# First rows and weights loaded ahead of the filter, and TensorE's dummy matmuls on a preset constant

## The chip, the core and the metric

The kernel runs on one core of a Trainium2 chip. The metric is the time of one execution on the device in microseconds (us). A core has TensorE (PE in the profile; its weight loads are PEld), VectorE (DVE), ScalarE (ACT), GpSimd (POOL) and SyncE (SP). SP and ACT issue the DMAs, which 16 DMA engines carry out.

## The reference

```
x  = A_q                                   # 2048 rows of 512, bf16
xn = layernorm(x)
k_shift = sum over 4 taps of shifted k * shift_k
kv = k_shift * v
y  = causal convolution of kv with ssm_k along the 2048 rows, by FFT of length 4096
y  = y + kv * ssm_D
s  = xn * y
g  = silu( (gelu(xn @ w_gate) * (xn @ w_up)) @ w_down )    # 512 -> 1792 -> 512
out = x + s * g
```

## The kernel before

**Tiling.** The 2048 rows are held as 16 tiles of 128 rows (X), in four quarters q of four tiles. Each quarter goes through layernorm (`ln(q)`: stats, aggregate, variance, a power on POOL, normalise into XN), a transpose into xnT (`xn_transpose(q)`), 14 feed-forward units (`unit(q, m)`: four gate and four up matmuls, gelu on ACT, a product on DVE into HT) and the down projection (`down(q)`). For quarter 0 the layernorm works tile by tile, and units 0 and 1 (`N_HALF = 2`) are split: matmuls of 128 columns on one row tile each, gelu and product on halves.

**The convolution** runs beside it, as a two-stage Fourier transform on PE. The filter `ssm_k` (Hn, four chunks h0 to h3) is transposed on PE (`h_transpose`, L915, in f32) into HTr, goes through stage 1 (L958) and is stored to a DRAM tensor ZH by ACT's queue, and reloaded as BH for stage 2 (L1027). The values kv go the same way (L949, ZK, BK). Spectra are multiplied on DVE, transformed back (L1027, ZI, BI, L1277), and joined to the result in the tail. The transform's tables (F, TF and their transposes) are computed at the start by POOL (iota), DVE (phases) and ACT (sine).

**Dummy matmuls.** `warm_up` issues `N_WARM` matmuls on a zeroed tile (ZERO, in AST) before PE has real work; their result is never read. The same step of DVE (`zero`) sets COLS, the bias of the sine, and clears ZERO, which a later small load (kz) also reads.

**Order.** Every step is a task with a number, in the order in which the program adds it. `SEQ` is a list written out by hand: it names the tasks in the order in which they are issued, each engine taking its own in that order; a `b` behind a number takes the second of two engines that could do the step (for copies out of PSUM, DVE in place of ACT). `Sched.run` only hands out buffers along that list, by estimated times; `LAND` holds the estimated landings of the loads. A recording layer (`Trk`) adds the semaphore waits. `ORDER` is the order in which SP issues the input loads: x00 and x01 are the first two pairs of row tiles, w0 the gate and up weights of units 0 and 1 (wg0, wu0), D the row `ssm_D`, s0 the taps.

**Names that the prediction uses.** L614 is the DMA helper, L632 and L635 the copies out of PSUM on ACT and DVE, L641 every plain matmul (dummies, gate, up, down), L671 to L689 POOL's iotas and identity matrices, L695 and L696 the two memsets of `zero`, L720 to L734 DVE's table phases, L744 and L748 the sine, and the gelu table behind it, L848 the stats, L849 the aggregate, L858 and L859 the variance on ACT or DVE, L861 the power on POOL, L870 the normalise step on DVE, L891 the transposes of XN, L915 those of the filter.

Of the kernel before, what the change touches and what calls it, by code (L numbers as in the profile page):

```python
# [6 lines left out]
BF16 = mybir.dt.bfloat16  # L7
# [14 lines left out]
NB = 2  # L22
LN_EPS = 1e-5
TURN = 8192
N_WARM = 12
ORDER = "x00 h0 x01 w0 D0 h1 w1 h2 h3 s0 k0 w2 x1 k1 k2 w3 d0 d1 v0 v1 k3 v2 v3 x2 x3"
SEQ = (
# [22 lines left out]
)  # L50
NF_BANKS = 4
ISSUE = 470.0
LAND = {"x0_0": 4400, "h0": 5900, "x0_1": 7000, "D": 4000, "wg0": 7950, "wu0": 8800, "h1": 10100, "wg1": 11600, "wu1": 13100, "h2": 14450, "h3": 15750, "sk": 17800, "kh1": 19200, "kh113": 19400, "kz": 10800, "k0": 20600, "wg2": 22500, "wu2": 24050, "x1": 25400, "k1": 26750, "k2": 28100, "wg3": 29650, "wu3": 31200, "wd0": 33450, "wd1": 35700, "v0": 37050, "v1": 38400, "k3": 39750, "v2": 41100, "v3": 42450}
W_XT, W_SW, W_BK, W_BH, W_ZI, W_BI, W_ZK, W_MI, W_G1 = 765000, 735000, 667000, 688000, 274000, 714000, 690000, 329000, 150000
NC_PAIRS = 4
SMALL = 1.15 * 262144
# [25 lines left out]
class Trk:  # L82
# [29 lines left out]
    def res(self, name, ap):  # L112
        t = ap.tensor
        tn = type(t).__name__
        if tn.startswith("SB"):
            key = "SB"
            addr = self.nc.lookup_mloc(t).addr
        else:
            assert tn.startswith("PS")
            key = "PS:" + t.name  # L120
            addr = 0
        esz = mybir.dt.size(ap.dtype)
        pairs = [list(q) for q in ap.ap]
        pst, pn = pairs[0]
        pstart = ap.offset // pst if pst else 0
        inner = ap.offset - pstart * pst
        hi = sum(st * (n - 1) for st, n in pairs[1:])
        r = Res(name, key, pstart, pstart + pn, addr + inner * esz, addr + (inner + hi + 1) * esz)
        lst = self.res_by_key.setdefault(key, [])
        for o in lst:  # L130
            if o.plo < r.phi and r.plo < o.phi and o.blo < r.bhi and r.blo < o.bhi:
                o.ovl.append(r)
                r.ovl.append(o)
        lst.append(r)
        return r
# [278 lines left out]
def build_kernel(nc, A_q, A_k, A_v, A_shift_k, A_ssm_k, A_ssm_D, B_w_gate, B_w_up, B_w_down, out):  # L414
    with ExitStack() as es0:
# [100 lines left out]
        trk = Trk(nc, block)  # L516
        S = Sched()
        res = trk.res

        def dsem(name):  # L520
            return DSem(nc.alloc_semaphore(name), name)
# [4 lines left out]
        def bank(b):  # L526
            return PSALL[:, 512 * b.slot:512 * (b.slot + 1)]
# [4 lines left out]
        def R_bank(b):  # L532
            return [R_ps[b.slot // 2][b.slot % 2]]
# [79 lines left out]
        def dma(eng, out_ap, in_ap, sem, r, w):  # L613
            trk.dma(eng, lambda e: e.dma_start(out=out_ap, in_=in_ap), sem, r=r, w=w)  # L614
# [3 lines left out]
        def load(name, out_ap, in_ap, w_res, w_buf, nbytes, ring="SP", r=(), rb=()):  # L618
            sem = dsem("d_" + name)
            last_load[0] = S.add([("loads", ISSUE)], lambda e: dma(ring, out_ap, in_ap, sem, r, w_res), r=rb, w=w_buf, nbytes=nbytes, land=float(LAND[name]))  # L620

# [18 lines left out]
        def mm(h, o, l, r, st, sp):  # L640
            return h.matmul(o, lhsT=l, rhs=r, start=st, stop=sp)  # L641
# [9 lines left out]
        bF1, bG1, bMF, bMI, bid, bSKB = B("F1"), B("G1"), B("TF"), [B(f"MI{i}") for i in range(2)], B("id"), [B(f"SKB{j}") for j in range(4)]  # L651
# [39 lines left out]
        ZERO = AST[:, 0, 0, 0, :]  # L691
        R_zero = res("ZERO", ZERO)
        bwarm = B("warm")
# [2 lines left out]
            trk.op("DVE", lambda h: h.memset(ZERO, 0.0), w=[R_zero])  # L696
        t_zero = S.add([("DVE", 330.0)], zero, w=[bwarm])
        warm = B("pswarm", pF)

        def warm_up(e):  # L700
            for i in range(N_WARM):
                trk.op("PE", lambda h: mm(h, bank(warm), ZERO[:, 0:128], ZERO, True, True), r=[R_zero], w=R_bank(warm), accum=True)

        t_warm = S.add([("PE", 10 * 427.0 + (N_WARM - 10) * 217.0)], warm_up, r=[bwarm], w=[warm])
        bcq, bck, bid32 = B("cq"), B("ck"), B("id32")
        S.add([("POOL", 420.0)], lambda e: pool_q(), w=[bcq])
        S.add([("POOL", 1000.0)], lambda e: pool_k(), w=[bck])
# [47 lines left out]
        bFP, bQ, bMQ, bMF2 = B("fp"), B("q"), B("mq"), B("mf2")  # L755
# [2 lines left out]
        S.add([("DVE", 360.0)], lambda e: f_phase(), r=[bFM], w=[bFP])  # L758
        def f_sin(e):
            sin(F1[:], C32[:].rearrange("p a c -> p (a c)"), [R_C32], R_F1)  # L760
        S.add([("ACT", 510.0)], f_sin, r=[bFP, bcq], w=[bF1])
        S.add([("DVE", 800.0)], lambda e: m_parts(), r=[bcq], w=[bQ])
        bTAB = B("tab")
        t_mq = S.add([("DVE", 900.0)], lambda e: m_phase(), r=[bQ, bck], w=[bMQ])
# [70 lines left out]

        for what in ORDER.split():
            if what[0] == "x" and len(what) == 3:
# [87 lines left out]
        for k in range(KD):  # L925
# [4 lines left out]
                    r=[bHD, *[bHTr[k][0] for k in range(KD)]], w=[bFold], rr=[R_D, *R_HTr[0]], ww=R_HTr[0])  # L930
# [369 lines left out]
        for j in range(6):  # L1300
# [7 lines left out]
                  r=[b2], w=[B(f"out{j}")], nbytes=262144)  # L1308
# [55 lines left out]
```

## Time and profile before

| | us |
|---|---|
| median of 3 runs | 188.87 (188.80 to 188.93) |
| profiled execution, its own time | 189.08 |
| span of its profile, first to last instruction | 187.3 |
| PE busy | 182.4 (97%) |
| DVE busy | 164.9 (88%) |
| ACT busy | 141.1 (75%) |
| POOL busy | 10.9 (6%) |

A line of the timeline is: start in us, duration in us, engine, source line, operation, tile written <- tiles read, shape, count of equal instructions merged, and in brackets how long the engine stood idle before it and what ended that. The duration of a merged line runs from the first start to the last end. A line of the chain holds start, duration and what it was. Ends of matmuls are modelled, so starts are what PE's rows are read by. A line of DMA issues ends with the size and the median time from issue to landing.

### The profile page before, as it was taken

Reading aid. Unit: us, or ns where it says so; the run is one execution under the profiler, and the core shown is the slowest. Engines: PE = TensorE matmul, PEld = TensorE weight load, DVE = VectorE, ACT = ScalarE, POOL = GpSimd, SP = SyncE. Lnnn points to the kernel's source line nnn. Section 1 sums busy time; section 2 is a strip of 40 time slices with the busy share of each in tenths; the row PEclk is TensorE's granted clock in tenths of the full one; section 3 lists DMA queues with packets and bytes.
Section 4 is the critical chain, followed back from the end, with each engine's and each line's share of the span. In section 5 each row is a group of like instructions: output and inputs, shape, how many; then the busy total and the mean of one; then the engine's idle time right before and its main releaser. Section 6 shows DMA issues by size and latency. Waiting matters only on the chain.

```text
span 187.3 us, 3717 instructions
## 1 busy us (share of the span) xinstructions
PE 182.4 (97%) x1474; PEld 81.5 (44%) x1474; DVE 164.9 (88%) x250; ACT 141.1 (75%) x196; POOL 10.9 (6%) x26
## 2 busy tenths in 40 slices
PE   7899999999999999999999999999999999999993
PEld 2675544534343334334444433433343344445552
DVE  7899999999999999978689689998999972759695
ACT  3847896997879799799638897998999663424871
POOL 5401402000000000022000000000000000000000
PEclk9999999999999999999999999999999999999999
DMA  5999999999584986457989997499445163995056
GB/s 188 318 381 294 371 379 365 400 411 319 163 321 159 336 290 223 158 195 238 311 244 233 321 332 240 153 304 307 182 168 168 60 216 123 321 392 187 0 205 243
DMA packets 36422, 47.84 MB, mean 255 GB/s; under 512 B 7347, under 2 KB 26039, under 8 KB 36406
## 3 DMA queue, kind: packets, MB, share of 16 engines
q1 hardware_dynamic: 29878, 39.23, 62.8%
q10 hardware_dynamic: 6528, 8.39, 13.0%
q8 instruction: 11, 0.18, 0.4%
q14 instruction: 5, 0.04, 0.2%
HBM read 27.39 MB, written 14.68 MB: 225 GB/s over the span
## 4 chain that ended last, share of the span: by engine, by line
PE 90%; DVE 4%; DMA 3%; issue 0%; SPq 0%; ACT 0%
PE psall L641 73%; PE psall L1027 6%; PE psall L1223 3%; DMA X<-in_A_q_dram 3%; PE psall L949 2%; PE psall L958 2%; PE psall L915 2%; PE psall L1277 1%; DVE G L1306 1%; DVE G L1245 1%; DVE G L1244 1%; PE psall L891 1%; DVE G L1294 1%; SPq L614 0%; DVE XN L1294 0%
## 5 line engine op out<-in xcount | busy, mean ns | idle before, releaser
L641 PE MATMUL psall<-xnT,Wu 128*128 128x512 bf16 (+1 forms) x248 | 55.8, 359 | 0.0
L641 PE MATMUL psall<-xnT,Wg 128*128 128x512 bf16 (+1 forms) x248 | 55.1, 359 | 0.7 <-DVE xnT L635 0.7
L641 PE MATMUL psall<-Wd,HT 128*128 128x512 bf16 (+1 forms) x182 | 40.6, 368 | 0.0
L1193 ACT ACTIVATE GE<-psall 128x512 bf16<-128x512 f32 x54 | 31.4, 604 | 12.1 <-PE psall L641 11.3
L1202 DVE TENSOR_TENSOR HT<-psall,GE 128x512 bf16<-128x512 f32 x43 | 29.0, 687 | 11.0 <-PE psall L641 10.8
L641 PEld LDWEIGHTS psall<-xnT,Wu 128*128 128x128 bf16 x248 | 22.5, 98 | 25.9 <-issue 2.3
L641 PEld LDWEIGHTS psall<-xnT,Wg 128*128 128x128 bf16 x248 | 21.7, 98 | 27.0 <-issue 2.3
L632 ACT ACTIVATE BO<-psall 128x1024 bf16<-128x1024 f32 x22 | 22.1, 1023 | 9.3 <-PE psall L1277 4.3
L641 PEld LDWEIGHTS psall<-Wd,HT 128*128 128x128 bf16 x182 | 16.1, 98 | 20.9 <-issue 3.7
L1130 DVE TENSOR_TENSOR HSW<-KB,HSW 128x2048 bf16<-128x2048 bf16 x16 | 19.2, 1218 | 0.0
L632 ACT ACTIVATE HSW<-psall 128x1024 bf16<-128x1024 f32 x16 | 15.5, 1035 | 2.3 <-PE psall L1027 2.2
L632 ACT ACTIVATE KB<-psall 128x1024 bf16<-128x1024 f32 x14 | 13.8, 1028 | 2.6 <-PE psall L1027 2.4
L1010 DVE TENSOR_TENSOR KAC<-KAC,KTM 128x2048 bf16<-128x2048 bf16 x12 | 14.7, 1224 | 0.1
L1008 DVE TENSOR_TENSOR KTM<-KK,SKB 128x2048 bf16<-128x2048 bf16 x12 | 14.7, 1222 | 0.1
L632 ACT ACTIVATE AST<-psall 128x1024 bf16<-128x1024 f32 x12 | 12.3, 1024 | 1.9 <-PE psall L949 1.5
L1223 PE MATMUL psall<-Wd,HT 128*64 128x512 bf16 (+1 forms) x112 | 12.3, 366 | 0.0
L848 DVE BATCH_NORM_STATS2 stats<-X 128x6 f32<-128x512 bf16 x16 | 10.6, 672 | 0.2
L1130 DVE TENSOR_TENSOR KB<-KB,HSW 128x2048 bf16<-128x2048 bf16 x8 | 9.6, 1219 | 0.1
L1153 DVE TENSOR_TENSOR HSW<-HSW 128x2048 bf16<-128x2048 bf16 x8 | 9.5, 1219 | 0.0
L1234 ACT ACTIVATE G<-psall 128x512 bf16<-128x512 f32 x12 | 6.9, 599 | 3.2 <-PE psall L641 3.2
L861 POOL TENSOR_TENSOR mv<-mv,NHALF 128x1 f32<-128x1 f32 (+1 forms) x7 | 5.3, 756 | 68.7 <-DVE mv L859 65.0
L1236 DVE SCALAR_TENSOR_TENSOR G<-G,psall 128x512 bf16<-128x512 bf16 x12 | 8.0, 681 | 1.2 <-ACT G L1234 1.2
(91 smaller groups left out, 177.8 us busy)
## 6 DMA issues: line engine op xcount, KB each, us to landing
BH<-ZH SPq DMA_DIRECT2D x8, 512.0 KB, 5.6
BK<-ZK SPq DMA_DIRECT2D x8, 512.0 KB, 6.1
HSW<-HSW SPq DMA_DIRECT2D x16, 256.0 KB, 3.4
ZI<-BO ACTq DMA_DIRECT2D x16, 256.0 KB, 2.6
BI<-ZI SPq DMA_DIRECT2D x8, 512.0 KB, 7.4
ZK<-AST SPq DMA_DIRECT2D x6, 512.0 KB, 3.4
Hn<-in_A_ssm_k_dram SPq DMA_DIRECT2D x4, 512.0 KB, 7.3
KK<-in_A_k_dram SPq DMA_DIRECT2D x4, 512.0 KB, 10.7
```

Of the source, the lines that this page charges most:

```text
L632: return h.activation(o, i, ACTF.Copy, scale=scale)
L641: return h.matmul(o, lhsT=l, rhs=r, start=st, stop=sp)
L848: t_stats[t] = op([("DVE", 670.0)], lambda e, h, t=t: h.bn_stats(stats[:, t, :], X[:, t, :]), r=[bX[q][t % 4]], w=[bst[t]], rr=[R_X[t]], w ...
L1008: op([("DVE", dur)], lambda e, h, j=j, m=m: h.tensor_tensor(KTM[:, m.slot, :, :], kk(j), sk(j), ALU.mult), r=need + [bSKB[j], a], w=[m], r ...
L1010: op([("DVE", dur)], lambda e, h, m=m: h.tensor_tensor(KAC[:, a.slot, :, :], KAC[:, a.slot, :, :], KTM[:, m.slot, :, :], ALU.add), r=[m], ...
L1027: trk.op("PE", lambda h: h.matmul(ps(s, i)[b, :], lhsT=wt(col)[a, :], rhs=data(col)[a, :], start=n < 16, stop=n >= len(todo) - 16, tile_po ...
L1130: return hd.tensor_tensor(pair(KB, *(2 * DM * z for z in slots())) if to else x, k, x, ALU.mult)
L1153: return hd.tensor_tensor(x, x, y, ALU.add)
L1193: op([("ACT", act(512))], lambda e, h: h.activation(GE[:, g.slot, :], bank(pg), ACTF.Gelu_apprx_tanh), r=[pg], w=[g], rr=lambda: R_bank(pg ...
L1202: op([("DVE", dve(512, 1))], lambda e, h: h.tensor_tensor(HT[:, q % 2, m, :], bank(pu), GE[:, g.slot, :], ALU.mult), r=[pu, g], w=[bHT[q][m]],
L1223: trk.op("PE", lambda h, m=m, i=i, c=c: h.matmul(pc()[c, :], lhsT=HT[:, q % 2, m, 128 * jt + 64 * i:128 * jt + 64 * i + 64], rhs=Wd[:, m, ...
L1236: op([("DVE", dve(512, 1))], lambda e, h, g=g, pc=pc: h.scalar_tensor_tensor(out=g, in0=g, scalar=1.0, in1=pc(), op0=ALU.add, op1=ALU.mult ...
```

## The change

The loads are issued as x00, x01, w0, D, h0, w1, h1, h2, h3 instead of x00, h0, x01, w0, D0, h1, w1, h2, h3; from the taps on the order is the same. The dummies read a constant tensor of ones, one value on each partition, read 512 and 128 times by a step of 0; the program's preamble sets it before the engines are released, so they wait for no step of DVE. There are 13 of them instead of 12. The sine of table F now names the memset of COLS among the steps that it follows. `LAND` takes new estimates, and the first 260 of `SEQ`'s 816 entries stand in a new order; from `120 180 160 141 162 119 121 129 545` on it is the old list.

What the new list does to the engines' programs, up to there: PE goes from the dummies to the transposes of the first two row tiles, to gate and up of units 0 and 1 on the first of them, and comes to the filter's transposes afterwards, in seven groups of four or eight instead of six. DVE begins with L720, then does the memsets and the other table steps, and takes the stats of the third tile between the normalise steps of the first and the second. DVE copies three PSUM tiles fewer (8 instead of 11 plain copies) and computes one variance fewer; ACT takes them (197 activations instead of 193). Four of ACT's filter stores (ZH), not two, stand ahead of the copies of the second quarter's transposes. On POOL the bf16 identity comes before the f32 one; on SP the transpose of F comes before that of the first half of TF.

```
-N_WARM = 12
-ORDER = "x00 h0 x01 w0 D0 h1 w1 h2 h3 s0 k0 w2 x1 k1 k2 w3 d0 d1 v0 v1 k3 v2 v3 x2 x3"
+N_WARM = 13
+ORDER = "x00 x01 w0 D0 h0 w1 h1 h2 h3 s0 k0 w2 x1 k1 k2 w3 d0 d1 v0 v1 k3 v2 v3 x2 x3"
 SEQ = (
-    "0 2 3 16 1 17 18 10 4 6 48 19 20 5 21 7 22 23 8 9 24 25 26 11 49 27 28 29 67 68 76b 30 31 32 65 66 73 12 77 78 74 75 69 87 91 86 90b 365 366 70 79b 71 "
+    "2 7 0 8 3 9 10 11 16 4 17 65 66 5 67 1 68 6 76 73b 74 75 12 86 69 18 77 78 90 87 365 70 377 79b 19 71 367 72 91 80 20 379 82b 378 81 381 21 366 88 92 "
...
-LAND = {"x0_0": 4400, "h0": 5900, "x0_1": 7000, "D": 4000, "wg0": 7950, "wu0": 8800, "h1": 10100, "wg1": 11600, "wu1": 13100, "h2": 14450, "h3": 15750, ...
+LAND = {"x0_0": 3800, "h0": 8050, "x0_1": 4900, "D": 6750, "wg0": 5850, "wu0": 6700, "h1": 12450, "wg1": 9600, "wu1": 11100, "h2": 13800, "h3": 15150, ...
...
+        ONE = nc.const_aps.tensor(1.0, [128, 512], BF16)
 
         def warm_up(e):
             for i in range(N_WARM):
-                trk.op("PE", lambda h: mm(h, bank(warm), ZERO[:, 0:128], ZERO, True, True), r=[R_zero], w=R_bank(warm), accum=True)
-
-        t_warm = S.add([("PE", 10 * 427.0 + (N_WARM - 10) * 217.0)], warm_up, r=[bwarm], w=[warm])
+                trk.op("PE", lambda h: mm(h, bank(warm), ONE[:, 0:128], ONE, True, True), w=R_bank(warm), accum=True)
+
+        t_warm = S.add([("PE", N_WARM * 427.0)], warm_up, w=[warm])
...
-        S.add([("ACT", 510.0)], f_sin, r=[bFP, bcq], w=[bF1])
+        S.add([("ACT", 510.0)], f_sin, r=[bFP, bcq, bwarm], w=[bF1])
```

Task numbers in the quoted lines: 0 `zero`, 1 the dummies, 7 and 8 DVE's L720 and L723, 10 and 11 the other phases, 9 and 12 the sines, 16 on the loads, 48 to 55 the filter's transposes and their copies, 65 to 84 the layernorm of quarter 0, 86 to 93 its transposes and copies, 365 on the units.

More of the change, by code (lines that the diff above doesn't have):

```diff
@@ L52 @@
 ISSUE = 470.0
-LAND = {"x0_0": 4400, "h0": 5900, "x0_1": 7000, "D": 4000, "wg0": 7950, "wu0": 8800, "h1": 10100, "wg1": 11600, "wu1": 13100, "h2": 14450, "h3": 15750, "sk": 17800, "kh1": 19200, "kh113": 19400, "kz": 10800, "k0": 20600, "wg2": 22500, "wu2": 24050, "x1": 25400, "k1": 26750, "k2": 28100, "wg3": 29650, "wu3": 31200, "wd0": 33450, "wd1": 35700, "v0": 37050, "v1": 38400, "k3": 39750, "v2": 41100, "v3": 42450}
+LAND = {"x0_0": 3800, "h0": 8050, "x0_1": 4900, "D": 6750, "wg0": 5850, "wu0": 6700, "h1": 12450, "wg1": 9600, "wu1": 11100, "h2": 13800, "h3": 15150, "sk": 17800, "kh1": 19200, "kh113": 19400, "kz": 10800, "k0": 20600, "wg2": 22500, "wu2": 24050, "x1": 25400, "k1": 26750, "k2": 28100, "wg3": 29650, "wu3": 31200, "wd0": 33450, "wd1": 35700, "v0": 37050, "v1": 38400, "k3": 39750, "v2": 41100, "v3": 42450}
 W_XT, W_SW, W_BK, W_BH, W_ZI, W_BI, W_ZK, W_MI, W_G1 = 765000, 735000, 667000, 688000, 274000, 714000, 690000, 329000, 150000
```

42 rows, old and new, of the table SEQ are left out of this document.

## The prediction

> **What bounds the kernel now.** I read the page first, for the shares of the chain, then the table by stages, then the timeline of the first 22 us, the chain piece by piece, and the issues of DMAs. PE is TensorE.
>
> ```profile
> span 187.3 us, 3717 instructions
> ...
> PE 90%; DVE 4%; DMA 3%; issue 0%; SPq 0%; ACT 0%
> ```
>
> ```profile
> 0.00:8.00 8.00, 6.04 (x31) 3.13 (x32) 6.38 (x23) 4.39 (x8) 3.81 (x17) 1.00 0.74 233
> 23.00:60.00 37.00, 36.97 (x193) 15.62 (x190) 36.97 (x52) 32.01 (x49) 1.02 (x1) 1.00 0.90 319
> 60.00:168.00 108.00, 108.00 (x960) 43.63 (x959) 92.01 (x124) 83.37 (x112) 2.03 (x2) 1.00 0.73 239
> ```
>
> Each row of the table holds a stretch, its length, then the busy time of PE, PE's weight loads, VectorE (DVE), ScalarE (ACT) and GpSimd (POOL), PE's granted clock, the DMA engines' share and GB/s. PE is on 90% of the chain; it is idle for 2 us of the first 8, and from 23 to 168 us it misses 0.03. Its work there is the same in both kernels, so what PE loses or saves in the front goes to the end, unless another engine takes it up; DVE is just as full from 23 to 60 us. I therefore count "lost" time: the start of PE's useful work, plus its waits after that.
>
> **The front now.** Rows of the timeline (start, duration):
>
> ```profile
> 0.79 0.06 DVE L695 MEMSET COLS<- 128x1 f32 x1 [0.79 <-PEq L1349]
> 0.91 0.18 POOL L672 IOTA K<- 128x64 int32 x1
> 1.21 4.37 PE L641 MATMUL psall<-AST 128*128 128x512 bf16 x12 [1.21 <-DVE Q L726]
> 1.78 0.68 DVE L720 TENSOR_SCALAR C<-K,Q 128x64 int32<-128x64 int32 x2
> 2.98 0.54 POOL L686 TENSOR_SCALAR ident<-K 128x128 bf16<-128x128 int32 x1
> 3.36 0.24 DVE L734 TENSOR_SCALAR PH<-PH 128x128 int32<-128x128 int32 x1
> 3.74 0.69 DVE L848 BATCH_NORM_STATS2 stats<-X 128x6 f32<-128x512 bf16 x1
> 3.74 0.15 PEld L641 LDWEIGHTS psall<-AST 128*128 128x128 bf16 x1 [0.28 <-issue]
> 4.17 0.15 PEld L641 LDWEIGHTS psall<-AST 128*128 128x128 bf16 x1 [0.28 <-issue]
> 4.47 0.18 DVE L849 BATCH_NORM_AGGREGATE mv<-stats 128x2 f32<-128x6 f32 x1
> 4.55 0.53 PEld L641 LDWEIGHTS psall<-AST 128*128 128x128 bf16 x3 [0.23 <-issue]
> 4.57 0.66 DVE L848 BATCH_NORM_STATS2 stats<-X 128x6 f32<-128x512 bf16 x1
> 4.68 0.30 ACT L858 ACTIVATE mv<-mv,EPSC 128x1 f32<-128x1 f32 x1 [1.48 <-DVE mv L849]
> 5.29 1.28 ACT L748 ACT_TABLE_LOAD   x1
> 5.41 1.04 PE L915 MATMUL psall<-ident,Hn 128*128 128x128 f32 x8
> 5.67 0.41 DVE L870 TENSOR_SCALAR XN<-X,mv 128x512 bf16<-128x512 bf16 x1
> 6.29 0.88 PE L891 MATMUL psall<-ident,XN 128*128 128x128 bf16 x8
> 6.31 0.41 DVE L870 TENSOR_SCALAR XN<-X,mv 128x512 bf16<-128x512 bf16 x1 [0.22 <-POOL mv L861]
> 6.72 0.60 ACT L632 ACTIVATE xnT<-psall 128x512 bf16<-128x512 bf16 x1
> 6.78 0.23 PEld L891 LDWEIGHTS psall<-ident,XN 128*128 128x128 bf16 x4 [0.27 <-DVE XN L870]
> 7.83 1.07 PE L641 MATMUL psall<-xnT,Wg 128*128 128x128 bf16 x16 [0.66 <-DVE xnT L635]
> 8.74 1.06 PE L641 MATMUL psall<-xnT,Wu 128*128 128x128 bf16 x16
> ```
>
> Useful work begins at 5.41 with transposes of the filter (Hn). A matmul of 128 columns takes 0.057 (16 of them from 7.83 to 8.74), so four transposes take 0.22. PE then waits for the second normalised row tile (6.51 to 6.78, 0.27) and for its transposed copy (7.00 to 7.83, 0.83). Lost: 5.41 + 0.27 + 0.83 = 6.51 us.
>
> **The change part by part.**
>
> *Dummies from the first moment.* DVE is released at 0.79, so I let PE start near 0.8, not 1.21. Weight loads of early dummies are 4.17 - 3.74 = 0.43 apart; the last four dummies go from 4.55 to 5.41, 0.216 each, so the fast pace begins 3.34 after the start. Thirteen dummies end between 0.8 + 8 x 0.43 + 5 x 0.216 = 5.3 and 0.8 + 13 x 0.43 = 6.4. Useful work cannot begin before 6.1 (next step), so the earlier start buys nothing; cost 0, at most 0.3. The constant that they read is set before the engines are released, so no wait is left.
>
> *The filter behind the rows.* In the new order of PE the first useful instruction is the transpose of the first row tile; the eight Hn transposes that filled PE from 5.41 are gone from there. That tile needs stats (3.74), aggregate, variance, power and normalise (5.67 to 6.08). None of these starts sooner: DVE now runs L720 first, which waits for K (0.91 + 0.18 = 1.09) where the table steps used to start at 0.79 and last to 3.36 + 0.24 = 3.60. With nothing regained they end at 3.9, and stats start at 3.74 to 3.95; I take 3.74, the row's own value, because the old order too held L720 back to 1.78, and keep 0.2 for the range. PE starts at 6.08 + 0.06 (as 6.78 stands behind 6.72) = 6.14.
>
> *Order on DVE.* The third stats now stand between the two normalise steps. Steps that don't wait for each other overlap by 0.08 (4.57 against 4.47 + 0.18): 6.08 - 0.08 + 0.69 - 0.08 + 0.41 = 7.02, where the second tile was ready at 6.31 + 0.41 = 6.72. PE takes it at 7.08, having idled from 6.36, 0.72. Its transposes end at 7.30. The first gate matmuls need the first tile's copy, which ACT can't begin before 6.72: the table load (5.29 to 6.57) and one small step stand ahead of it in both orders. It ends at 7.32; gate work starts at 7.38. Lost: 7.38 - 2 x 0.22 = 6.94. **Front: +0.43.** From there I find no further wait: 16 gate and up matmuls on the first tile (0.9) last to 8.3, where the second copy (ACT, behind one variance step of 0.30: 7.6 to 8.2) is there.
>
> *Rows and weights first.* The second rows landed at 6.74:
>
> ```profile
> 1.64 5.10 DMA X<-in_A_q_dram
> ```
>
> Now they are issued second, with 256 KB ahead of them instead of 768, and DVE wants them at 6.0. In the old order DVE had work up to 6.72, so the early landing saves it 0.04 and no more, until DVE comes to them sooner. The first weights used to land before the gate rows at 7.83 and 8.74 and now have 512 KB less ahead of them. The first filter chunk now stands where the first up chunk stood in bytes, in time for 8.74; PE reaches it at about 9.2. SP's other loads keep their places. On POOL the two identity matrices swap; both are ready by 3.52 now, far ahead of 6.1. On SP the transposes of F and TF swap; they feed work behind 100 us. No cost.
>
> *Filter transposes later.* Beginning them behind 128-column matmuls costs PE a restart:
>
> ```profile
> 9.87 0.71 PE L915 MATMUL psall<-ident,Hn 128*128 128x128 f32 x4
> 10.64 0.66 PE L915 MATMUL psall<-ident,Hn 128*128 128x128 f32 x4
> 16.15 1.11 PE L915 MATMUL psall<-ident,Hn 128*128 128x128 f32 x8
> 18.81 0.71 PE L915 MATMUL psall<-ident,Hn 128*128 128x128 f32 x4
> 21.09 0.60 PE L915 MATMUL psall<-ident,Hn 128*128 128x128 f32 x4
> ```
>
> Behind a 512-column matmul four take 0.60 (21.09); the others cost 0.11, 0.06, 0.07 (1.11 against 1.04 at 5.41) and 0.11 more, 0.35 in all. The new order has seven groups, four of them behind 512 columns: 3 x 0.06 to 0.11. **-0.12** (-0.17 to 0).
>
> *The order behind.* Up to about 50 us it is new on PE, DVE and ACT. PE has two small waits there now:
>
> ```profile
> 25.84 1.03 PE L641 MATMUL psall<-xnT,Wu 128*128 128x512 bf16 x4
> 26.83 1.47 PE L641 MATMUL psall<-xnT,Wg 128*128 128x512 bf16 x6
> 35.89 0.23 PEld L891 LDWEIGHTS psall<-ident,XN 128*128 128x128 bf16 x4 [0.20 <-ACT XN L869]
> ```
>
> Four matmuls at 0.216 would bring the next at 26.70, so 0.13 is lost there, and up to 0.20 at 35.89. They may go (-0.33) or come back elsewhere (0). DVE is as full as before; I take **-0.1**, nearer to 0.
>
> *Sum:* 0.43 - 0.12 - 0.1 = +0.21 us; the span goes to 187.5. The profiled execution took 189.08 (span 187.3 and 1.8 around it), 0.21 above the median of 188.87; so 189.29 for it, **189.1 us** for the median. From the bounds, this case alone lies between 188.8 (all lower ends: 0.43 - 0.17 - 0.33) and 189.5 (0.43, and 0.2 for later stats).
>
> A difference of 0.2%, 0.38 us, is about what a measurement tells from no change.
>
> **Rivals.**
>
> A, faster. The first rows land sooner without 512 KB right behind them, and DVE's table steps end by 3.4; then the whole front moves 0.35 forward, and with the lower ends above the sum is 0.43 - 0.35 - 0.17 - 0.33 = -0.42: 188.5 us. For: DVE was free at 3.60 and stats began at 3.74, so the rows came last. Against: DVE's steps now start later.
>
> B, slower. The new order gives ACT three copies out of PSUM that DVE had, and a variance step.
>
> ```profile
> 57.45 0.10 PEld L949 LDWEIGHTS psall<-V,F 64*128 64x128 bf16 x2 [0.35 <-ACT U__74 L632]
> ```
>
> At 57 us PE's weight load already waited for ACT, just short of stopping PE. Three copies at 0.60 to 1.02 are up to 3.1 us more for ACT, which idles 37 - 32.01 = 5.0 from 23 to 60. It decides once ACT stands about 0.4 later against PE there than now; half a copy, 0.5, then lands on PE: 189.6 us.
>
> C, the clock. After 5.3 PE works 0.44 us out of 2.1. If it falls back to the 0.43 pace for as long as the rise took (3.34), half of that is lost: 190.8 us. Against: after 7.00 it waited 0.83 and went on at 0.057 a matmul. The granted clock can't tell: it reads 1.00 for the first 8 us, half-paced dummies included. [...]
>
> D, loads. Four filter stores (ZH) of 512 KB stand ahead of the next quarter's copies on ACT, two before. At the 319 GB/s of 23 to 60 us two more are 3.3 us of queue among the loads.
>
> ```profile
> 20.24 6.64 SPq L614 DMA_DIRECT2D Wd<-in_B_w_down_dram  x2
> Wd<-in_B_w_down_dram SPq DMA_DIRECT2D x2, 896.0 KB, 14.3
> 39.83 1.04 PE L641 MATMUL psall<-Wd,HT 128*128 128x512 bf16 x4
> ```
>
> The first lands at 20.24 + 14.3 = 34.5 and is used from 39.83, so 5 us cover it; the second, issued some 3 us later, has about 2 to 3. If those are used up, PE waits up to 1: 190.1 us.
>
> **Chances.** Forecast 0.50, A 0.15, B 0.20, C 0.05, D 0.10. Faster by over 0.2% takes most of A: 0.12. Within it: two thirds of the forecast, the rest of A and the mildest of B and D: 0.42. Slower: the upper third of the forecast and most of B, C and D: 0.46. The range from 188.45 to 190.1 leaves out half of A, C, and half of D, about 0.17.
>
> **What would show it.** Right: first dummy near 0.75, row transposes at 6.1 and 7.1, gate work at 7.4, Hn behind it, and all PE rows near 60 us 0.2 later than now. Wrong: first stats before 3.5 (A), PE waits between 50 and 60 us (B), gate matmuls 0.11 apart (C), or Wd matmuls behind a DMA (D).

## The result, and the profile after

The changed kernel takes 190.12 us (median; 189.66 to 190.57), the kernel before in the same session 189.02: a ratio of 1.0051, 95% interval 1.0033 to 1.0069, so 0.6 to 1.3 us slower. The forecast was 189.1. The profiled execution of the changed kernel is the slowest of its own runs, 190.57, 1.49 above the profiled one of before.

The page's span and shares of the chain, and the table by stages (columns as before):

```profile
span 188.8 us, 3718 instructions
...
PE 76%; DMA 11%; DVE 6%; ACT 4%; issue 1%; POOL 0%; POOLq 0%; ACTq 0%
```

```profile
23.00:60.00 37.00, 36.34 (x188) 15.26 (x187) 36.04 (x52) 31.26 (x46) 1.93 (x1) 1.00 0.87 312
60.00:168.00 108.00, 107.64 (x958) 43.28 (x956) 92.84 (x125) 83.74 (x112) 2.03 (x2) 1.00 0.74 233
```

PE's share of the chain has fallen from 90% to 76%, and DMA has 11%. From 23 to 60 us, where PE missed 0.03 before, it misses 0.66; from 60 to 168 us it misses 0.36, which is the wait for BK at 91 us below. From 23 to 60 us neither DVE nor ACT is fuller than before (36.04 and 31.26 instead of 36.97 and 32.01). Something between them waits.

The front, from the timeline:

```profile
0.76 5.12 PE L641 MATMUL psall<-const-bfloat16-1.0 128*128 128x512 bf16 x13 [0.76 <-PEq L1350]
3.65 0.69 DVE L849 BATCH_NORM_STATS2 stats<-X 128x6 f32<-128x512 bf16 x1
6.11 0.40 PE L892 MATMUL psall<-ident,XN 128*128 128x128 bf16 x4 [0.22 <-DVE XN L871]
...
6.66 0.58 ACT L632 ACTIVATE xnT<-psall 128x512 bf16<-128x512 bf16 x1
7.02 0.40 PE L892 MATMUL psall<-ident,XN 128*128 128x128 bf16 x4 [0.52 <-DVE XN L871]
7.29 0.62 PE L641 MATMUL psall<-xnT,Wg 128*128 128x128 bf16 x8
```

All of it stands within 0.1 us of the times that were forecast. PE's useful work begins at 6.11; it then loses 7.02 - 6.34 = 0.68 and 7.29 - 7.24 = 0.05, 6.84 in all beside 6.51 before. So the front costs 0.33, about a third of the loss. The rest is further back, on the chain of waits from 30 to 49 us (start, duration, what):

```profile
30.78 9.55 DMA ZH<-X
...
40.35 1.02 ACT X L632
41.37 0.49 ACT U__74 L632
41.86 0.50 ACT xnT L632
...
42.40 0.39 PE psall L959 x2
...
44.33 1.03 ACT XN L632
45.36 0.49 ACT G L1235
45.85 0.98 ACT xnT L632 x2
...
46.88 1.90 PE psall L641 x8
```

A filter store (ZH) that ACT issued at 30.78 lands at 40.33. ACT's next copy of the filter's first stage goes into the same staging buffer, in X, and waits for that:

```profile
40.35 1.02 ACT L632 ACTIVATE X<-psall 128x1024 bf16<-128x1024 f32 x1 [1.21 <-DMA ZH<-X]
41.69 0.39 PE L959 MATMUL psall<-HTr,F 64*128 64x512 bf16 x2
42.40 0.39 PE L959 MATMUL psall<-HTr,F 64*128 64x512 bf16 x2 [0.33 <-ACT xnT L632]
43.81 0.61 PE L892 MATMUL psall<-ident,XN 128*128 128x128 bf16 x8
44.50 2.12 PE L641 MATMUL psall<-Wd,HT 128*128 128x512 bf16 x9
46.88 1.47 PE L641 MATMUL psall<-xnT,Wg 128*128 128x512 bf16 x6 [0.26 <-ACT xnT L632]
```

Behind the waiting copy stand U and xnT, which PE needs. Two L959 matmuls, one pair, take 0.22 (a row of two lasts 0.39, one of four 0.61), so 0.49 is lost from 41.69 to 42.40; eight transposes take 0.45, so 0.24 from 43.81 to 44.50; nine matmuls at 0.216 take 1.94, so 0.44 from 44.50 to 46.88. That is 1.17 us by the starts; the table's 0.66 is less because the modelled ends of the matmuls in front of each wait cover part of it. A fourth wait, for BK at 91 us, adds 0.4 in this profile; it is taken up with the transposes of SP below.

### The profile page after: what moved, and what is told of

The parts are those of the page before. It is cut to its first block, busy times and chain, and to the rows that moved or that the text cites. A ratio compares the mean times of both kernels' runs of the same rounds, so it can differ in the third digit from the quotient of the medians.

```text
span 188.8 us, 3718 instructions
## 1 busy us (share of the span) xinstructions
PE 183.4 (97%) x1475; PEld 81.4 (43%) x1475; DVE 162.5 (86%) x246; ACT 143.7 (76%) x200; POOL 11.5 (6%) x26
## 3 DMA queue, kind: packets, MB, share of 16 engines
q10 hardware_dynamic: 6528, 8.39, 12.7%
## 4 chain that ended last, share of the span: by engine, by line
PE 76%; DMA 11%; DVE 6%; ACT 4%; issue 1%; POOL 0%; POOLq 0%; ACTq 0%
PE psall L641 60%; DMA ZH<-X 5%; PE psall L1028 5%; DMA BK<-ZK 4%; PE psall L1224 3%; PE psall L916 2%; PE psall L950 2%; DMA ZK<-AST 2%; PE psall L959 2%; PE psall L1278 1%; DVE G L1307 1%; ACT AST L632 1%; DVE G L1246 1%; DVE G L1245 1%; ACT xnT L632 1%
## 5 line engine op out<-in xcount | busy, mean ns | idle before, releaser
L641 PE MATMUL psall<-xnT,Wu 128*128 128x512 bf16 (+1 forms) x248 | 56.5, 359 | 0.0
L1194 ACT ACTIVATE GE<-psall 128x512 bf16<-128x512 f32 x54 | 31.4, 604 | 12.9 <-PE psall L641 12.1
L862 POOL TENSOR_TENSOR mv<-mv,NHALF 128x1 f32<-128x1 f32 (+1 forms) x7 | 6.2, 891 | 68.5 <-DVE mv L860 65.5
L632 ACT ACTIVATE X<-psall 128x1024 bf16<-128x1024 f32 x8 | 8.2, 1028 | 2.0 <-DMA ZH<-X 1.2
```

Of the source, the lines that this page charges most:

```text
L632: return h.activation(o, i, ACTF.Copy, scale=scale)
L1194: op([("ACT", act(512))], lambda e, h: h.activation(GE[:, g.slot, :], bank(pg), ACTF.Gelu_apprx_tanh), r=[pg], w=[g], rr=lambda: R_bank(pg ...
```

## The experiments

Two theories. **Store:** the loss is the wait for the buffer of the store, the front is small. **Front:** the loss is the later start of useful work and its order, and the waits at 41 to 47 us are its echo. Ratios are to the kernel before, run beside each on the same chip, where its median was 189.24 to 189.40.

**A fifth staging buffer.** The first stage has four of them, two in XN and two in X. The order of every engine stays as in the changed kernel.

```
- ast = {"H": [T[:, 4 * j:4 * j + 4, :]... for T in (XN, X) for j in (2, 3)],
+ ast = {"H": [T[:, 4 * j:4 * j + 4, :]... for T in (XN, X) for j in (2, 3)] + [AST[:, 1, :, :, :]],
```

> The changed kernel with a fifth staging buffer for the filter's first stage (a second one in AST, idle until 55 us), so that no copy needs the buffer whose store (ZH<-X, issued at 30.78) lands only at 40.3. Store theory: ACT no longer waits 1.2 us ahead of its copy into X near 40 us, PE's waits at 41.7, 44.2 and 46.2 us (0.50, 0.24 and 0.42 over the pace of its matmuls, 1.16 in all) are gone, the wait for BK at 92 us shrinks with them, and the time is 188.8 to 189.2 us, within 0.2 of the kernel before. Front theory (the loss is the later start of useful work and its order): the time stays at 190.1 us, and PE stands 1 us later at 54 us as in the changed kernel.

Measured: 189.26, ratio 0.9997 (0.9981 to 1.0013). Its timeline at the places of the three waits:

```profile
41.84 0.61 PE L959 MATMUL psall<-HTr,F 64*128 64x512 bf16 x4
42.38 1.25 PE L641 MATMUL psall<-Wd,HT 128*128 128x512 bf16 x5
43.47 0.61 PE L892 MATMUL psall<-ident,XN 128*128 128x128 bf16 x8
43.91 2.10 PE L641 MATMUL psall<-Wd,HT 128*128 128x512 bf16 x9
45.85 1.89 PE L641 MATMUL psall<-xnT,Wg 128*128 128x512 bf16 x8
```

All three are gone (0.44 for the eight transposes, 1.94 for the nine matmuls). The first matmuls of the values' transform show the sum; the rows are those of before, the changed kernel and the fifth buffer:

```profile
53.76 0.61 PE L949 MATMUL psall<-V,F 64*128 64x512 bf16 x4
```

```profile
54.75 0.61 PE L950 MATMUL psall<-V,F 64*128 64x512 bf16 x4
```

```profile
53.72 0.61 PE L950 MATMUL psall<-V,F 64*128 64x512 bf16 x4
```

PE stands 0.99 later than before in the changed kernel and 0.04 earlier with the fifth buffer. The two intervals of the ratio (1.0033 to 1.0069, 0.9981 to 1.0013) don't meet. By these rows the whole loss goes with the buffer; the time alone would still allow 0.25 us of it (0.13%) to be left. The store theory holds. One part of it fell: the wait for BK at 91 us was still there (0.27 by the row of that profile).

**The waiting copy put later**, no buffer added.

```
- ... 425 138 477 40 157 426 481 427 ...
+ ... 425 477 40 157 426 481 138 427 ...
```

> The changed kernel with one ACT step moved: the copy that waits for the store (task 138) stands behind the copies U and xnT that were queued behind it, no buffer added. Store theory: the wait still ends when the store lands, but U and xnT no longer stand behind it; of PE's three waits those at 41.7 and 44.2 us go (0.74), the one at 46.2 us stays (0.4): 189.2 to 189.5 us. Front theory: 190.1 us.

Measured: 189.92, ratio 1.0032 (1.0015 to 1.0050), 0.6 us over before and 0.4 above the expected range. The interval overlaps with that of the changed kernel, so the time does not show what the move gained; the profile does. One wait is left, where the fifth buffer had 45.85:

```profile
46.13 1.90 PE L641 MATMUL psall<-xnT,Wg 128*128 128x512 bf16 x8 [0.21 <-ACT xnT L632]
```

Its nine matmuls before it began at 43.82, so 0.37 is lost there, and the first L950 row stands at 54.00, 0.28 behind the fifth buffer and 0.75 ahead of the changed kernel. In these two profiles the price depended on what was queued behind the waiting step, as the store theory has it. Why the medians of this version and of the fifth buffer are 0.66 apart, and not 0.28, stays open.

**The price put into the kernel before**: its first two stores a few steps later on ACT, at 33.00 and 33.41 us. (In the trace of before they stand at 27.07 and 30.18; the 27.98 below is a misreading.)

```
- ... 461 117 419 466 421 462 104 105 410 ... 439 470 ...
+ ... 461 419 466 421 462 104 410 ... 439 117 105 470 ...
```

> The kernel before with one thing moved: ACT's first two filter stores, issued there at 27.98 and 30.18 us, stand behind six and four more of ACT's own steps, so that they are issued near 32.5 us; PE, DVE and the loads keep their orders. Store theory: a store that is issued among the last input loads takes up to 9.5 us to land (9.55 in the changed kernel), so these land near 42 us; ACT's copies of the first filter stage into the same buffers (39.78 and 42.56 us in the kernel before) wait for that, 1 to 2.4 us, and PE behind them waits 1 to 1.9 us near 43 to 44 us: 190.2 to 191.2 us. Rival (the landing of a store has cover enough, the loss in the changed kernel came with its own order): within 0.2 us of the kernel before.

Measured: 191.08 in four runs, ratio 1.0095 (1.0069 to 1.0121). The chain of its profile:

```profile
33.00 8.51 DMA ZH<-XN
...
41.60 1.03 ACT XN L632
42.66 1.03 ACT XN L632
...
43.73 0.39 PE psall L958 x2
```

It is the same chain in the old order: store, copy, PE. PE lost 0.55 there in this profile, less than expected; 0.86 more was lost in its front (gate work at 8.69 instead of 7.83) for another reason, the dummies' pace, below. So the mechanism is shown, and only part of the 1.7 us is its price; how large a part in the median stays open.

Why do these stores take so long? Of four filter stores in the changed kernel issued from 21 to 38 us, the landings took 7.8, 9.5, 12.7 and 10.0 us; of the four issued from 49 us on, when the input loads were in (the last landed at 47.2), 2.8 to 4.0. The two queues from 30.8 to 40.3 us (packets, MB, share of 16 engines; q1 is SP's, q10 ACT's), while the engines moved 385 GB/s on average:

```profile
q1 hardware_dynamic: 1816, 2.74, 81.8%
q10 hardware_dynamic: 453, 0.89, 24.4%
```

The loads took three bytes of four, and from 30.8 to 33.0 us ACT's queue moved nothing. How the engines share their time between the two queues is not shown beyond these figures. That the loads are the reason for the long landings is read from these landings alone; no run changed the loads around a store.

**The third stats behind the second normalise step**, with the fifth buffer.

```
- ... 12 86 69 18 77 78 90 ...
+ ... 12 86 18 77 78 69 90 ...
```

> The kernel with the fifth buffer, with DVE's third stats put behind the second normalise step of quarter 0. By the prediction's third step (the stats between the two steps cost the front 0.43): PE's transposes of the second row tile come at 6.7 us instead of 7.0, gate work at 6.9 to 7.3, and the time is up to 0.3 us below that with the fifth buffer alone. Rival: ACT's first copy (6.66 to 7.24 us) sets the gate work in any order, and the third and fourth tiles' stats come 0.4 later, so that PE waits for their normalised rows near 8.3 and 8.9 us: 0.3 to 0.4 us above the fifth buffer alone.

Measured: 189.25, ratio 1.0001 (0.9984 to 1.0018). Rows of its profile, then of the fifth buffer alone:

```profile
6.83 0.40 PE L892 MATMUL psall<-ident,XN 128*128 128x128 bf16 x4 [0.18 <-DVE XN L871]
7.44 0.62 PE L641 MATMUL psall<-xnT,Wg 128*128 128x128 bf16 x8 [0.21 <-ACT xnT L632]
9.06 0.40 PE L892 MATMUL psall<-ident,XN 128*128 128x128 bf16 x4
```

```profile
7.17 0.40 PE L892 MATMUL psall<-ident,XN 128*128 128x128 bf16 x4 [0.52 <-DVE XN L871]
7.44 0.62 PE L641 MATMUL psall<-xnT,Wg 128*128 128x128 bf16 x8
8.79 0.39 PE L892 MATMUL psall<-ident,XN 128*128 128x128 bf16 x4
```

The second tile comes 0.34 sooner, gate work at the same 7.44, and the third tile 0.27 later. ACT's first copy sets the gate work in either order. The time doesn't tell the two apart.

**The dummies alone**, in the kernel before: 13 on the preset constant.

> The kernel before with the dummies alone changed: 13 on the preset constant, from 0.76 us. Prediction's first step: they end by 5.3 to 5.7 us, the filter's transposes begin at 5.4 to 5.7, PE waits for the first copy of xnT at 7.83 as before, and the time stays within 0.2 us of 189.0. Rival (clock): the fast pace comes only 4.4 us after the first dummy, at 5.2 us, as in the changed kernel and later than the 4.55 of the kernel before, and part of the transposes runs at half pace: they end past 7.0 us, gate work comes 0.1 to 0.5 later, up to 189.5 us.

Measured: 189.57, ratio 1.0015 (0.9995 to 1.0035), which doesn't decide. Rows of its profile:

```profile
0.76 5.48 PE L641 MATMUL psall<-const-bfloat16-1.0 128*128 128x512 bf16 x13 [0.76 <-PEq L1349]
6.08 1.05 PE L915 MATMUL psall<-ident,Hn 128*128 128x128 f32 x8
7.59 0.69 DVE L848 BATCH_NORM_STATS2 stats<-X 128x6 f32<-128x512 bf16 x1 [0.86 <-DMA X<-in_A_q_dram]
8.66 1.07 PE L641 MATMUL psall<-xnT,Wg 128*128 128x128 bf16 x16 [1.09 <-DVE xnT L635]
```

From the first dummy to the filter's transposes 5.32 us pass, where 13 dummies at 0.427 would make 5.55. So the fast pace came only with the last of them, later still than the rival has it, and the transposes begin at 6.08 instead of 5.41. Gate work is 0.83 later than in the first profile of before, but the pace is not what set it: DVE waited 0.86 for the second rows, which landed late, and its copy for the gate work stands behind that. The profile therefore bears out neither forecast. A late pace is also no mark of the constant, since the dummies on zeroes have it in some executions. Beside the 12 in 4.37 us of the prediction's row stand another profile of before, and that of before with the late stores:

```profile
1.20 4.78 PE L641 MATMUL psall<-AST 128*128 128x512 bf16 x12 [1.20 <-DVE Q L726]
```

```profile
1.21 5.30 PE L641 MATMUL psall<-AST 128*128 128x512 bf16 x12 [1.21 <-DVE Q L726]
8.69 1.07 PE L641 MATMUL psall<-xnT,Wg 128*128 128x128 bf16 x16 [0.52 <-DVE xnT L635]
```

The first of these is the kernel before, unchanged:

> The kernel before, unchanged, for another profile: at which time the dummies reach the fast pace (3.34 us after the first in its first profile, 2.9 to over 5.2 us in those of the changed front), and whether PE waits for BK at 91 us (0.34 to 0.45 us in four profiles of the changed order, nothing in two of the old). If the pace comes by a clock of the chip's own, its time differs here too; if the wait at 91 us belongs to the changed order, there is none here.

It took 188.97, with no wait at 91 us.

**The order of the loads alone**, in the kernel before.

> The kernel before with the new order of the loads alone (and its estimates of their landings); every engine's program is otherwise the old one, so PE still begins with the filter's transposes. By the landings in the changed kernel the filter's first chunk is there at 8.6 us instead of 5.1: PE starts useful work at 8.7 instead of 5.4, the row tiles' transposes stand behind that, and gate work comes near 10.5 instead of 7.83: 191.5 to 192.2 us. Rival (prediction: the order of the loads costs nothing by itself): 189.0 to 189.4 us.

Measured: 192.98, ratio 1.0186 (1.0157 to 1.0216).

```profile
8.33 1.14 PE L915 MATMUL psall<-ident,Hn 128*128 128x128 f32 x8 [1.95 <-DMA Hn<-in_A_ssm_k_dram]
10.67 0.61 PE L641 MATMUL psall<-xnT,Wg 128*128 128x128 bf16 x4 [0.52 <-DVE xnT L635]
```

Gate work comes at 10.67 instead of 7.83, and the time is 0.7 longer still. In this profile PE's matmuls run slower for a while, and the granted clock is low there. The page's row of the granted clock, in tenths in slices of 4.8 us, has a dip at the third slice:

```profile
PEclk9969999999999999999999999999999999999999
```

In finer windows it reads 0.50 from 9.5 to 12.9 us. The 16 gate matmuls take 1.68 there, from 10.67 to 12.35, instead of 0.91 (0.105 apart instead of 0.057), and the 16 up matmuls 1.18 instead of 0.89. PE had been idle for 1.95 us at a stretch and no longer. So the order of the loads was cheap here only together with PE's new order.

**The transposes of SP put back**, with the fifth buffer.

```
- ... 153 178 179 120 180 ...
+ ... 153 179 178 120 180 ...
```

> The kernel with the fifth buffer, with one thing put back: SP transposes the first half of TF ahead of F, as in the kernel before (near 32 to 50 us). It asks where PE's wait for BK near 91 us (0.34 to 0.45 in four profiles of the changed order, where BK took 7.3 to 7.4 us to land; none in the old order, where it took 3.9 to 6.1) comes from. If the order of these transposes on SP and the DMA engines decides it: BK lands in 4 to 6 us, no wait at 91 us, and the time is 0.3 us below that with the fifth buffer alone, 188.9 to 189.0 us beside 189.25. Rival (it comes with something else in the changed order): BK again takes 7.3 us and the time is that with the fifth buffer.

Measured: 189.45, ratio 1.0013 (0.9994 to 1.0033), no gain. BK took 6.9 us and PE came to it at 91.25 without a wait in this profile; in that of the changed kernel it was this:

```profile
92.72 0.44 PE L1028 MATMUL psall<-BK,TF 32*32 32x512 bf16 x16 [0.36 <-DMA BK<-ZK]
```

Here the wait is missing and the time no better, so it isn't what separates the kernels. Why BK took 6.9 to 7.4 us in the five profiles that keep the new front's order, 3.9 to 6.1 in those of the old order and 5.0 to 5.6 in the two tries below, stays open.

**Two tries at a version that beats both**, each with the fifth buffer, 12 dummies and small moves among the first 285 entries of the order.

> The changed kernel with the fifth buffer, 12 dummies instead of 13, and the first 285 entries of the order moved by a few places each, so that two groups of the filter's transposes that stand alone are joined to others (one restart of PE less, 0.1) and the rest packs more tightly. Expected from the rows: 0.1 for the restart, 0.15 where the last dummy still ran at 6.1 us: 188.9 to 189.1 us, 0.1 to 0.3 under the kernel before. Rival (the waits in front are set by the normalisation of the rows, and nothing is to be had): the same as the kernel before, 189.2 us.

Measured: 197.28, ratio 1.0390 (1.0359 to 1.0422). The moves had also changed the order of the loads, which was not meant: the first gate and up weights were issued ahead of the first rows, and DVE waited for those (not for the second rows, as the text on the next try has it).

```profile
7.32 0.69 DVE L849 BATCH_NORM_STATS2 stats<-X 128x6 f32<-128x512 bf16 x1 [3.79 <-DMA X<-in_A_q_dram]
```

PE's first useful matmul comes at 9.73, 3.5 later than with the fifth buffer, after 3.85 us without work. The granted clock is then 0.50 from 9.0 to 15.8 us, and at the first stage of the filter (23.12 instead of 17.40) PE is 5.7 behind. The last 2 us of the 7.7 by which the span is longer were not followed.

> The changed kernel with the fifth buffer, the transposes of SP as in slot5_swap, 12 dummies, and the first 285 entries of the order moved by a few places each, this time with the loads in the changed kernel's own order (in best, the second rows had come behind the first weights, and DVE waited 3.8 us for them). The filter's transposes stand in six groups instead of seven (0.1), and the last dummy ends by 6.05 us at either pace (0.15 where the pace came late): 188.7 to 189.1 us where the kernel before stands at 189.25. Rival: the new places bring a wait of their own of the same size, and it stands at 189.2 or above.

Measured: 189.15, beside 189.36 for the kernel before, ratio 0.9998 (0.9973 to 1.0022). It is no measurable gain. Here PE came to the filter's first chunk too soon:

```profile
9.38 1.14 PE L916 MATMUL psall<-ident,Hn 128*128 128x128 f32 x8 [0.20 <-DMA Hn<-in_A_ssm_k_dram]
```

No version here beats the kernel before by more than the measurement is uncertain.

## Why the prediction was right or wrong

Slower was the likeliest sign (0.46, beside 0.42 for no clear change), and it is slower; but the forecast's reason, the front, carries a third of it. The forecast was a change of 0.21, the measured one is 0.96 by the ratio. From the 188.87 that the forecast started with, that is 189.8, 0.7 above the forecast and inside the range; the median of its own session, 190.12, is 1.0 above it and just past the upper end. That this is where rival D had put it is luck, because the price came another way.

- *Dummies from the first moment* (cost 0, at most 0.3). They began at 0.76 and were over before the first row tile's transposes at 6.11. With the pace late, as in the profile of the fifth buffer, those came at 6.26, but there the stats began 0.14 later too (3.79), and PE waited for the rows that DVE normalised. So even a late pace cost this front nothing that shows. Right.
- *The filter behind the rows.* Stats at 3.65 (forecast 3.74), first transposes at 6.11 (6.14). Right. Rival A needed stats before 3.5 and is out: DVE's table steps ended at 3.73.
- *Order on DVE.* 7.02 (7.08) and 7.29 (7.38), 0.33 lost instead of 0.43. The size was right. That ACT's copy sets the gate work was right too; the stats moved back gained nothing.
- *Rows and weights first* (no cost). True beside PE's new order, +3.6 us without it.
- *Filter transposes later* (-0.12). The seven groups took 0.66, 0.66, 0.66, 0.60, 0.60, 0.62 and 1.05: 0.21 of restarts instead of 0.35, so -0.14. Right.
- *The order behind* (-0.1, from -0.33 to 0). This is the step that failed. Both old waits went, -0.33, the lower end. But three new ones came, +1.17, and the step had no upper end above zero. It asked which waits go and not which the new order brings.

With the parts that were right, 0.33 - 0.14 - 0.33 = -0.14, and the fifth buffer's profile, whose first stats came 0.14 later, stands at -0.04 against before. The new waits make up the rest: -0.14 + 1.17 = 1.03 beside 0.99 measured at 54 us.

Rival D had the premise: four stores ahead of the next quarter's copies, among the loads. It sent the price to the loads, and there the cover held: no Wd matmul waits for a DMA, though the last load lands 2.8 us later than before (47.2 instead of 44.4). The price came from the stores' own landing, through the four staging buffers, which the prediction didn't count. Rival B had the place where it hurts: ACT, which PE waits for. It looked at ACT's busy time from 50 to 60 us, where nothing happened; ACT lost its time waiting at 39 us with less work than before (31.26 of 37 us instead of 32.01).

Rival C did not happen in the changed kernel: gate matmuls in its front are 0.057 apart. But with the order of the loads alone the granted clock did fall, to 0.50, and gate matmuls ran 0.105 apart, where PE had idled for 1.95 us at a stretch and no longer. With the copy put later PE idled 0.89 and 0.52 us in its front by its rows, and eight gate matmuls behind that took 0.45 (7.37 to 7.82), 0.056 each. What brings the fall no run shows.

The early stores were in the list of the change and the four buffers in the code, and the trace of before held a warning: ACT waited once for such a store there (0.59 us ahead of its copy at 46.53 us, without PE waiting). Following each early store to the next writer of its buffer would have found the wait.

## What to carry to other kernels

When an order is changed, follow each transfer that moves earlier to the next step that writes its buffer, and take its landing time from transfers issued among the same traffic, not from the median (here 7.8 to 12.7 us among the loads, where the page's medians for these stores are 5.9 and 6.3). A waiting step cost here what was queued behind it on its engine: in the profiles a spare buffer removed the whole loss of 0.99 us at 54 us, a later place for the step 0.75 of it. Pieces of a found order (loads, front, dummies) did not have prices of their own here: the new order of the loads cost 3.6 us alone, and no wait with the new order of PE.

## What the runs showed of the hardware that was not expected

**The pace of the dummies.** In the profiles of before, dummies ran 0.427 apart until 3.3 or 4.2 us after the first one, and then 0.216; with late stores, over 5 us passed with no change. In the changed front it was 3.3 us with the copy put later, 4.5 in the changed kernel, and over 5 in the five others. The data and the kernel don't decide it: on zeroes it was 3.3, 4.2 and over 5 us, on ones 3.3, 4.5 and over 5. What does decide it no run shows. The profile's granted clock does not show the change of pace: it reads 1.00 in the first 8 us of before and of the changed kernel alike, with dummies 0.427 apart in both.

It bears on fronts. In the kernel before PE's first useful work follows the dummies. With the pace later than the dummies (before with late stores) the filter's transposes began at 6.30 instead of 5.41 and gate work at 8.69 instead of 7.83. In the changed front PE waits for the normalised rows in any case: gate work came at 7.44 to 7.47 in the three profiles of its front with the pace over 5 us, and at 7.29 and 7.37 in the two others. But the first stats, too, began later in the three (3.79 to 3.82) than in the two (3.65 and 3.71). This is the row with the fifth buffer:

```profile
3.79 0.69 DVE L849 BATCH_NORM_STATS2 stats<-X 128x6 f32<-128x512 bf16 x1
```

So the rows alone account for the difference, and the new front lost nothing to a late pace that shows. How often the pace comes late in either kernel was not measured, so what this is worth in the medians stays open.

**A granted clock that fell.** With the order of the loads alone the granted clock fell to 0.50 at 9.5 us and stood there for 3.4 us, after no idle stretch longer than 1.95 us. Unlike the slow pace at the start, this does show in the profile's row of the clock. The 32 gate and up matmuls there took 2.86 us instead of 1.80.
